# Attention and experts on one core: gate logits of two tiles one round later, loads held to their round, and the last tiles' copies put ahead of the routing work

## The chip, the core and the metric

The kernel runs on one core of one Trainium2 chip. The metric is the device time of one execution in microseconds (us). Three runs of the kernel before took 263.19, 261.66 and 264.2 us, median 263.19.

The engines are named as in the profile: PE multiplies matrices (PEld is its weight load), DVE is the vector engine, ACT the scalar engine, POOL is GpSimd, SP issues nearly all transfers. Each works through its own instructions in order.

## The reference

Attention with a window, then a mixture of experts over its output:

```
scores = q @ k^T / 8;  keep = key < 8  or  0 <= query - key < 96
scores = where(keep, scores - slope[head] * distance, -1e9)
x = softmax(scores) @ v                      # 4 batches x 8 heads x 768 x 64
logits = x @ w_gate                          # 3072 tokens x 8 experts
e = argmax(logits); gate = softmax(logits)[e]
per expert: keep the 80 tokens of highest gate
out[token] = gate * (relu(x @ w1[e]) @ w2[e]);  all other rows of out are zero
```

All data is float32; w1 is 8 x 512 x 1024, w2 is 8 x 1024 x 512.

## The kernel before, in words

**Attention** takes tiles of 128 queries (24 of them) in 48 rounds `u`, two per tile: a round has four heads. The loop over `u` in `fast_path` writes the order of all five queues out by hand (`manual_schedule`), so that what stands first in the code stands first in its engine's queue. In round u, in this order:

- `scores(u)`: PE multiplies q and k into `ring` (three PSUM buffers, two used per round, L180). Four times, DVE adds the bias and takes the extreme (`ts`, `nm`, L200), and ACT takes the exponential (`pwz`, L204). In between stand `transposes(u - 2)` on PE (into `tp`, L241 to L254, and ACT's copy of half of it to `ta`, L258), `invert(u - 1)` on DVE (`z`, L212 and L213) and `norm(u - 1)` on POOL (L221).
- `logits2` in every fourth round: two transposes (L329) of gate logits that DVE has copied to `ls`, and DVE's sums of them (L358).
- `copied(u - 2)`: DVE copies the other half of `tp` to `ta` (L264). From round 20 on SP then stores a finished piece of x to DRAM (L267).
- `logits1` in every fourth round: PE multiplies two finished tiles `ut` with the gate weights into `lps` (L317), and DVE copies that to `ls` (L321).
- `weigh(u - 3)`: PE multiplies `ta` with v into `pair` (L288, L297). After a tile's second round ACT copies `pair` to `ut` (L311). The next tile's first product overwrites `pair`, and so waits for that copy.
- loads of a later tile (`load_blk`: q and v; `keys`: k), weights and wipes by the table `ASKS`, and a few steps of `routes`: softmax and ranks of a group of tiles (the groups have 6, 6, 6, 4 and 2 tiles), nearly all on DVE. The largest step is `compare` (`cf`, L542).

So the tile pair's logits come right after the copy of its second tile: `logits1` in rounds with u % 4 = 3, `logits2` in rounds with u % 4 = 0.

q, v and k sit in buffers of four tiles (k of two batches). SP issues loads as soon as the buffer is free. A weight quarter (512 KB, `w`) has 16 buffers; the first use of one is held back by a write of one element on POOL (`G.memset(t[:1, :1], 0.0)`, L91), so that SP waits until POOL reaches it.

**The drain** (`DRAIN`) writes the end of the attention out step by step. `t46` and `t47` are transposes and copies of the last two rounds, `w44` to `w47` the products with v, `n47` the last normalisation (split over DVE and POOL by `NORM`), `a1` to `c3` the last logits, `r` a step of routing, `o` one wipe (512 KB of zeros to the output).

**Selection** (`select`) ranks the tokens, finishes x in DRAM and finds the 80 tokens of each expert. **Experts** then gathers them and runs 64 weight quarters through PE: each is split into a high and a low part (ACT L810, DVE L814), and each split asks for the next quarter's load, so that 16 are always held or under way. In `select` the order of SP is left to a scheduler, and it put two wipes that `select` asks for near the start of SP's queue, among the first loads.

Of the kernel before, what the change touches and what calls it, by code (L numbers as in the profile page):

```python
# [22 lines left out]
P = 128  # L23
NB = S // P
# [24 lines left out]

EARLY = "k12 q1 v0 k23 v1 q2 w0 v2"  # L50
ASKS = "- - - - - w ww w ww w w - w - w - w - w - w - www -".split()
HELD, EVERY, AFTER = 2, 3, 2
FROM, INSIDE = 18, 14


DRAIN = (
    "r a1 t45 o o w44 r r r n47 r r a2 t46 r r r r w45 r r r "
    "t47 w46 r b1 w47 r r b2 c1 c2 r r r c x x c3 c c r r y y"
)
NORM = (("V", slice(2, 4)), ("G", slice(0, 2)))  # L60
ROWS = (3, 1, 3, 1, 0, 0, 0)
# [9 lines left out]
def fast_path(tc, a, out, cst, x_dram, inp):  # L71
# [4 lines left out]
    with ExitStack() as ctx:  # L76
# [8 lines left out]
        def load_w():  # L85

            for n, (k, e, c) in enumerate(QUARTERS):
                t = wp.tile([P, DF], F32, tag="w", name=f"w{k}_{e}_{c}")
                raw[k, e, c] = t
                if n < NW:  # L90
                    G.memset(t[:1, :1], 0.0)  # L91
                src = (a["w1"] if k == 1 else a["w2"])[e].rearrange("(c p) f -> p c f", p=P)
                yield nc.sync.dma_start(out=t.rearrange("p (c f) -> p c f", c=k), in_=src[:, k * c:k * c + k])
# [46 lines left out]
        with tc.tile_pool(name="at_sb", bufs=2) as sp, ExitStack() as sctx:  # L140
# [19 lines left out]
            def scores(u):  # L160
                t, g = divmod(u, 2)
                m = TURN[t] % NB
                q, kt = inp.blk[t][0], inp.kts[TURN[t] // NB]
                nm, z, ts, pw = st[u]
# [96 lines left out]
            def copied(u):  # L261
                spot = u - FROM
                ta, tp, n = st[u, "ta"]
                V.tensor_copy(out=ta[:, 1, :n], in_=tp[:, :n])  # L264
                if 0 <= spot < 2 * INSIDE:
                    r = TURN[spot // 2] * P
                    nc.sync.dma_start(  # L267
                        out=x_dram[r:r + P, :].rearrange("p (i g c) -> p i g c", i=2, g=2)[:, :, spot % 2], in_=ta[:, :, n - P:n])
                st[u, "ta"] = ta

            def weigh(u):
                t, g = divmod(u, 2)
                m = TURN[t] % NB
                va, vb = inp.blk[t][1:]
                last = u == nu - 1
# [108 lines left out]
            weights = load_w()  # L384
            ahead = islice(weights, NW)
            wipe = clear()
# [3 lines left out]
            for u in range(nu - 1):  # L390
                if u % 2 == 0:
                    next(keys, None)
                if u == 0:
                    for _ in cst["first"]:
                        pass
                begin(u)
                scores(u)
                if u % 4 == 0 and 8 <= u:
                    logits2(u // 2 - 4, 2)
                if 2 <= u:  # L400
                    copied(u - 2)
                if u == 1:
                    for _ in window:
                        pass
                    for z in pwz:
                        G.memset(z[:, 4 * WH:], 0.0)
                    G.memset(cst["zero"], 0.0)
                if u > 2:
                    for _ in range(3):
                        next(late, None)  # L410
                if u % 4 == 3 and 7 <= u:
                    logits1((u - 7) // 2, 2)
                if 3 <= u:
                    idle(2 if u == 3 else 0)
                    weigh(u - 3)
                if u % 2 == 0 and 3 <= u // 2 + 2 < NT:
                    inp.load_blk(u // 2 + 2)
                if u % 2:
                    for k in ASKS[u // 2]:
                        next(dict(w=ahead, o=wipe).get(k, iter(())), None)  # L420
                routes(4 if u >= 40 else 2 + (u % 4 == 3))
            u = nu - 1
# [3 lines left out]
            def whole(u):  # L426
# [3 lines left out]
            step = dict(  # L430
                o=lambda: next(wipe),
                t45=lambda: copied(u - 2), t46=lambda: whole(u - 1), t47=lambda: whole(u),
                w44=lambda: weigh(u - 3), w45=lambda: weigh(u - 2), w46=lambda: weigh(u - 1), w47=lambda: weigh(u),
# [31 lines left out]
        early = [hip.tile([P, DF], F32R, tag="hi", name=f"early{i}") for i in range(3)]  # L465
        select(tc, cst, lps, psa, pair, gs1, rows, due, raw, early, wipe)
        pctx.close()
        rctx.close()
        assert next(ahead, END) is END
        experts(tc, out, cst, x_dram, inp, raw, weights, lps, early, hip, wipe)  # L470


class Route:
# [26 lines left out]
    def all(self):  # L500
        V, A, lg, ex, eq = self.nc.vector, self.nc.scalar, self.lg, self.ex, self.eq
        yield V.tensor_reduce(out=self.mx, in_=lg, axis=AX.X, op=ALU.min)
        yield V.tensor_tensor(out=ex, in0=self.wide(self.mx), in1=lg, op=ALU.subtract)
        yield V.tensor_tensor(out=eq, in0=lg, in1=self.wide(self.mx), op=ALU.is_equal)
        yield A.activation(out=ex, in_=ex, func=AF.Exp, bias=0.0, scale=1.0)
        yield V.tensor_tensor(out=eq, in0=eq, in1=self.cst["pref"].unsqueeze(1).broadcast_to([P, self.n, E]), op=ALU.mult)
        yield V.tensor_reduce(out=self.m2, in_=eq, axis=AX.X, op=ALU.max)
        yield V.tensor_reduce(out=self.sx, in_=ex, axis=AX.X, op=ALU.add)
# [200 lines left out]

def select(tc, cst, lps, psa, pair, gs1, rows, due, w, early, wipe):  # L710

# [9 lines left out]
    with tc.tile_pool(name="sel2", bufs=2) as s2, tc.tile_pool(name="ps_s", bufs=1, space=PSUM) as ps, \  # L721
            tc.manual_schedule(engines=ORDERED):
        duo = ps.tile([P, 2, 512], F32, name="duo")
# [18 lines left out]
        assert next(tiles, END) is END  # L742
        for _ in islice(wipe, AFTER):
            pass
# [35 lines left out]
def experts(tc, out, cst, x_dram, inp, raw, weights, lps, early, hip, wipe):  # L780
# [5 lines left out]
    with tc.tile_pool(name="ffn", bufs=2) as fp, tc.tile_pool(name="hl", bufs=NLO) as hl, \  # L786
# [143 lines left out]
        def prepare(n, behind=False):  # L930
            for k, e, c in islice(fill, n):
                ready[k, e, c] = split(raw.pop((k, e, c)), DF, f"w{k}_{e}_{c}", behind)
                next(weights, None)
                if nsplit % EVERY == 0:
                    next(wipe, None)

        with tc.manual_schedule(engines=ORDERED | {ET.SP}):
            targets(nc, cst)
            for e in range(E):
                gather(e)  # L940
                if e == 0:
                    prepare(1, True)
            nc.sync.dma_start(out=cst["scl"][:1], in_=xgs[0][:1, :2])
            for n in range(2):
                prepare(n)
# [380 lines left out]
class Inputs:  # L1326
# [37 lines left out]

    def load_q(self, t, ks=slice(0, NP * P)):
        self.nc.sync.dma_start(out=self.q[t % self.NQ][:, ks], in_=self.a["q"][TURN[t]][:, ks])

    def load_v(self, t):
        dma, n, m = self.nc.sync.dma_start, TURN[t], TURN[t] % NB
        va = self.va[t % self.NQ]  # L1370
        if m:
            vb = self.vb[t % self.NQ]
# [3 lines left out]
        else:  # L1376
            vb = None
            dma(out=va, in_=self.a["v"][n])
        self.blk[t] = (self.q[t % self.NQ], va, vb)

    def load_blk(self, t):
        self.load_q(t)
        self.load_v(t)

# [69 lines left out]
```

## Time and profile before

| | |
|---|---|
| median of three runs | 263.19 us |
| profiled execution | 262.77 us, of which the span from the first to the last instruction is 261.1 |
| attention, to the drain | 0 to 133 us |
| drain | 133 to 143.7 |
| selection | 143.7 to 159.8 |
| experts | 159.8 to 255.4 |
| busy | PE 239.1 us, DVE 213.8, ACT 206.1, POOL 105.9 |

The span's own engine totals say little, since the stages have different limits: in the experts PE is busy for 95.48 of 95.60 us, in the attention all of PE, ACT and DVE are busy for more than four fifths of the time. The rows are read by stage, and in the attention by round. A round is found in the trace by its four exponentials on ACT: round 8 begins at 27.7 us, round 24 at 70.9, round 40 at 114.7, so a round lasts 2.70 us in the first of these stretches and 2.74 in the second.

### The profile page before, as it was taken

The numbers are of one execution on the slowest core, as the hardware profiler recorded it, in microseconds if no ns is written. First come the engines' busy times: TensorE is split into PE (matmuls) and PEld (weight loads), VectorE is DVE, ScalarE is ACT, GpSimd is POOL, SyncE is SP. The second block draws the span as 40 slices with busy tenths as digits, with TensorE's granted clock in tenths as the row PEclk, the third lists the DMA queues.
The fourth block names the chain that finished last, engine by engine and source line by source line (L and its number), as shares of the span: only waits on it lengthen the run. The fifth ranks groups of instructions, "written<-read, shape, count | busy, mean of one in ns | idle before, by whom it ended". The sixth has DMA issues, their size and how long they took to land.

```text
span 261.1 us, 9657 instructions
## 1 busy us (share of the span) xinstructions
PE 239.1 (92%) x3587; PEld 168.7 (65%) x3587; DVE 213.8 (82%) x785; ACT 206.1 (79%) x583; POOL 105.9 (41%) x196
## 2 busy tenths in 40 slices
PE   7987988899998999998999889999999999999991
PEld 2565766667676786876766645666666666666660
DVE  4877677988878889787987778999999898999860
ACT  3988789999789998997985555888879898979740
POOL 7675565544445744555561438820000031111211
PEclk9999999999999999999999858999999999999999
DMA  5999639999979999898467646999999999999101
GB/s 172 293 353 319 189 103 312 346 334 316 314 226 302 284 259 300 264 283 271 154 195 274 246 158 201 342 326 403 405 407 410 410 401 395 391 407 336 34 25 36
DMA packets 49086, 73.06 MB, mean 280 GB/s; under 512 B 3688, under 2 KB 23528, under 8 KB 49032
## 3 DMA queue, kind: packets, MB, share of 16 engines
q1 hardware_dynamic: 47864, 69.74, 79.6%
q0 software_dynamic: 1024, 2.62, 3.2%
q8 instruction: 30, 0.49, 0.8%
q14 instruction: 24, 0.20, 0.2%
q10 hardware_dynamic: 144, 0.00, 0.0%
HBM read 58.46 MB, written 13.89 MB: 277 GB/s over the span
## 4 chain that ended last, share of the span: by engine, by line
PE 62%; ACT 18%; DVE 8%; issue 5%; POOL 4%; POOLq 0%; DVEq 0%; ACTq 0%
PE hp L840 17%; PE yp L840 17%; ACT pwz L204 11%; PE ring L180 6%; PE pair L288 6%; PE pair L297 3%; ACT ta L258 3%; ACT ut L311 2%; PE lps L317 2%; DVE ts L200 2%; PE tp L895 2%; PE tp L241 2%; PE lps L591 1%; POOL pwz L221 1%; DVE z L212 1%
## 5 line engine op out<-in xcount | busy, mean ns | idle before, releaser
L204 ACT ACTIVATE pwz<-ts,nm 128x168 f32<-128x168 f32 (+1 forms) x192 | 81.4, 426 | 14.8 <-DVE z L212 12.4
L221 POOL TENSOR_TENSOR pwz<-pwz,z 128x672 f32<-128x672 f32 (+2 forms) x48 | 60.3, 1257 | 56.6 <-DVE z L213 34.4
L200 DVE CUSTOM_DVE_ANT_0 ts<-ring,tab 128x168 f32<-128x168 f32 (+1 forms) x192 | 53.2, 315 | 14.4 <-PE ring L180 13.4
L180 PE MATMUL ring<-kt,q 64*64 64x64 f32 (+3 forms) x1088 | 41.1, 268 | 2.1 <-issue 1.0
L923 POOL DMA_INDIRECT out_dram<-vb,si x8 | 9.5, 1188 | 76.7 <-ACT w_0h L810 39.0
L204 ACT ACTIVATION_READ_ACCUMULATOR pwz<-ts,nm 128x1 f32 x192 | 36.6, 191 | 0.0
L180 PEld LDWEIGHTS ring<-kt,q 64*64 64x64 f32 x1088 | 32.4, 133 | 5.4 <-issue 2.9
L288 PE MATMUL pair<-ta,va 104*64 104x128 f32 (+1 forms) x368 | 30.6, 285 | 3.0 <-ACT ut L311 2.1
L264 DVE COPY ta<-tp 128x512 f32<-128x512 f32 (+2 forms) x47 | 28.7, 611 | 0.0
L288 PEld LDWEIGHTS pair<-ta,va 104*64 104x64 f32 (+1 forms) x368 | 19.3, 136 | 12.1 <-issue 6.3
L258 ACT COPY ta<-tp 128x512 f32<-128x512 f32 (+2 forms) x47 | 23.9, 508 | 0.5 <-ACT pwz L204 0.5
L241 PE MATMUL tp<-ident,pwz 64*128 64x64 f32 x376 | 21.9, 235 | 2.0 <-POOL pwz L221 1.4
L241 PEld LDWEIGHTS tp<-ident,pwz 64*128 64x128 f32 x376 | 15.5, 138 | 9.7 <-POOL pwz L221 4.3
L814 DVE TENSOR_TENSOR w_3l<-w,w_3h 128x1024 fp32r<-128x1024 f32 x16 | 19.5, 1221 | 1.4 <-ACT w_3h L810 1.2
L814 DVE TENSOR_TENSOR w_0l<-w,w_0h 128x1024 fp32r<-128x1024 f32 x15 | 18.3, 1221 | 2.0 <-ACT w_0h L810 2.0
L297 PE MATMUL pair<-ta,vb 64*64 64x64 f32 x640 | 18.8, 230 | 1.1 <-issue 1.1
L297 PEld LDWEIGHTS pair<-ta,vb 64*64 64x64 f32 x640 | 13.1, 133 | 8.1 <-issue 7.9
L814 DVE TENSOR_TENSOR w_1l<-w,w_1h 128x1024 fp32r<-128x1024 f32 x15 | 18.3, 1219 | 0.0
L814 DVE TENSOR_TENSOR w_2l<-w,w_2h 128x1024 fp32r<-128x1024 f32 x15 | 18.2, 1216 | 0.0
L810 ACT CAST w_3h<-w 128x1024 fp32r<-128x1024 f32 x16 | 16.7, 1044 | 0.3 <-PE yp L840 0.3
L810 ACT CAST w_2h<-w 128x1024 fp32r<-128x1024 f32 x15 | 15.8, 1056 | 1.2 <-PE hp L840 1.0
L200 DVE DVE_READ_ACCUMULATOR2_ANT nm<- 128x1 f32 x192 | 15.9, 83 | 0.0
(436 smaller groups left out, 521.9 us busy)
## 6 DMA issues: line engine op xcount, KB each, us to landing
w<-in_w_dram SPq DMA_DIRECT2D x64, 512.0 KB
kt<-in_kT_dram SPq DMA_DIRECT2D x23, 272.0 KB
out_dram<-zero SPq DMA_DIRECT2D x12, 512.0 KB
q<-in_q_dram SPq DMA_DIRECT2D x23, 256.0 KB
vb<-in_vb_dram SPq DMA_DIRECT2D x20, 256.0 KB
va<-in_va_dram SPq DMA_DIRECT2D x20, 208.0 KB
x_dram<-ta SPq DMA_DIRECT2D x28, 128.0 KB
x_dram<-kt SPq DMA_DIRECT2D x6, 256.0 KB
```

Source lines behind the costliest of these rows:

```text
L180: T.matmul(sc[hh][64 * i:64 * i + 64, pp, o:o + e - c], q[h, pr * P + 64 * i:pr * P + 64 * i + 64], kt[h, pr, c0 + c:c0 + e], start=True, ...
L200: V.tensor_tensor_reduce(out=ts[:, j, :w], in0=sc[hh][:, pp, :w], in1=tab, scale=-0.125, scalar=3.0e38, op0=ALU.add, op1=ALU.min, accum_ou ...
L204: A.activation(out=pw[:, j, :w], in_=ts[:, j, :w], func=AF.Exp, bias=nm[:, j:j + 1], scale=-1.0, accum_out=z[:, j:j + 1],)
L221: eng.tensor_tensor(out=p, in0=p, in1=zs.unsqueeze(2).broadcast_to(list(p.shape)), op=ALU.mult)
L241: T.transpose(out=tps[i][:, 64 * j:64 * j + 64], in_=pw[hs[i], o:o + P], identity=ident[hs[i], hs[i]])
L258: A.copy(out=ta[:, 0, :n], in_=tps[0][:, :n])
L264: V.tensor_copy(out=ta[:, 1, :n], in_=tp[:, :n])
L288: T.matmul(up[pp][64 * hh:64 * hh + 64], va[:n, 64 * h:64 * h + 64], ta[:n, :, 64 * j:64 * j + 64], start=g == 0 if t < NT - 1 else pp == ...
L297: T.matmul(up[pp][h, 64 * i:64 * i + 64], vb[k, i, 2 * g + pp, :], ta[k, i, 256 + 64 * pp:320 + 64 * pp], start=False, stop=True, skip_gro ...
L810: A.copy(out=hi, in_=src)
L814: V.tensor_tensor(out=lo, in0=src, in1=hi, op=ALU.subtract)
L840: T.matmul(ps, p, q, start=first and i == 0, stop=last and i == 2, skip_group_check=True)
```

## The change

- **Logits one round later.** `logits1` moves from rounds with u % 4 = 3 to those with u % 4 = 0, `logits2` from u % 4 = 0 to u % 4 = 1. The steps of routing that follow them move too: before, four steps were made in each round from 40 on; now five are made in each from 41 on.
- **Loads to their round.** Up to round 20, q and v of a tile are held by a write of one element on POOL, as weights are. v is asked for three rounds later than before (v of tile t in round 2t - 1), k after q instead of ahead of the scores (and, up to round 20, two rounds later).
- **Weights and wipes.** Weight quarters are asked for one at a time from round 5 on, every second round up to round 19, where before they began in round 11. Fourteen are loaded by the end of the drain, two more after the last rows of x; before, all sixteen were. The two wipes that stood near the start are now in rounds 23 and 31. In the experts the first split no longer asks for a quarter: the stream of quarters begins behind the first gather.
- **The drain.** ACT copies the second half of round 46 instead of DVE; the copies of rounds 46 and 47 stand ahead of the routing of the group of four; two small routing operations of that group move from DVE to POOL; the last normalisation has three heads on DVE and one on POOL, instead of two and two.

```diff
-EARLY = "k12 q1 v0 k23 v1 q2 w0 v2"
-ASKS = "- - - - - w ww w ww w w - w - w - w - w - w - www -".split()
-HELD, EVERY, AFTER = 2, 3, 2
+EARLY = "k12 q1 v0 k23 v1 q2 w0"
+ASKS = "- - w w w w w w w w - o - w - o - w - - w - - -".split()
+HELD, EVERY, AHEAD, LATE = 2, 3, 14, 2
+HOLD = 20
 DRAIN = (
-    "r a1 t45 o o w44 r r r n47 r r a2 t46 r r r r w45 r r r "
-    "t47 w46 r b1 w47 r r b2 c1 c2 r r r c x x c3 c c r r y y"
+    "w r w a1 t45 w o w44 o r r r n47 r r a2 t46 r r r w45 t47 r r r r w46 b1 r r r w47 b2 c1 c2 "
+    "r r r c x x c3 c c c r r y y"
 )
-NORM = (("V", slice(2, 4)), ("G", slice(0, 2)))
+NORM = (("V", slice(1, 4)), ("G", slice(0, 1)))
...
-                V.tensor_copy(out=ta[:, 1, :n], in_=tp[:, :n])
+                (A.copy if u == nu - 2 else V.tensor_copy)(out=ta[:, 1, :n], in_=tp[:, :n])
...
             for u in range(nu - 1):
-                if u % 2 == 0:
-                    next(keys, None)
...
-                if u % 4 == 0 and 8 <= u:
-                    logits2(u // 2 - 4, 2)
+                if u % 4 == 1 and 9 <= u:
+                    logits2((u - 9) // 2, 2)
...
-                if u % 4 == 3 and 7 <= u:
-                    logits1((u - 7) // 2, 2)
+                if u % 4 == 0 and 8 <= u:
+                    logits1((u - 8) // 2, 2)
...
                 if u % 2 == 0 and 3 <= u // 2 + 2 < NT:
-                    inp.load_blk(u // 2 + 2)
+                    inp.load_q(u // 2 + 2, hold=u < HOLD)
+                    for _ in range(1 + (u == 20)):
+                        next(keys, None)
                 if u % 2:
+                    if 2 <= u // 2 + 1 < NT:
+                        inp.load_v(u // 2 + 1, hold=u < HOLD)
...
-                routes(4 if u >= 40 else 2 + (u % 4 == 3))
+                routes(5 if u > 40 else 2 + (u % 4 == 3))
...
+        side = self.nc.gpsimd if self.t0 == NT - GROUPS[-2] - GROUPS[-1] else V
-        yield V.tensor_tensor(out=ex, in0=self.wide(self.mx), in1=lg, op=ALU.subtract)
+        yield side.tensor_tensor(out=ex, in0=self.wide(self.mx), in1=lg, op=ALU.subtract)
...
-        for _ in islice(wipe, AFTER):
+        for _ in late:
             pass
...
                 ready[k, e, c] = split(raw.pop((k, e, c)), DF, f"w{k}_{e}_{c}", behind)
-                next(weights, None)
+                if not behind:
+                    next(weights, None)
...
-    def load_q(self, t, ks=slice(0, NP * P)):
+    def load_q(self, t, ks=slice(0, NP * P), hold=False):
+        if hold:
+            self.nc.gpsimd.memset(self.q[t % self.NQ][:1, :1], 0.0)
```

How the orders move, at three places. On PE, in a round with u % 4 = 3 (round 23; `tp` are the transposes, `lps` the gate logits, `pair` the products with v, `ring` the next scores), before:

```order
L254 MATMUL tp_21_1606<-ident,ut_379 128x64
L254 MATMUL tp_21_1607<-ident,ut_379 128x64
L317 MATMUL lps<-ut_1368,wgn 32x256 x4
L288 MATMUL pair<-ta_1541,va 64x128 x4
L297 MATMUL pair<-ta_1541,vb_118 64x64 x8
L180 MATMUL ring_208<-kt_113,q_109 64x128
```

And of the change, in that round:

```order
L255 MATMUL tp_21_1618<-ident,ut_375 128x64
L255 MATMUL tp_21_1619<-ident,ut_375 128x64
L289 MATMUL pair<-ta_1554,va 64x128 x4
L298 MATMUL pair<-ta_1554,vb_118 64x64 x8
L181 MATMUL ring_206<-kt_113,q_109 64x128
```

The four logits products are gone from it: `pair` now follows the transposes at once. They stand in the next round, where the transposes of `ls` (L329) stood:

```order
L255 MATMUL tp_22_1681<-ident,ut_618 128x64
L255 MATMUL tp_22_1682<-ident,ut_618 128x64
L318 MATMUL lps<-ut_1375,wgn 32x256 x4
L289 MATMUL pair<-ta_1620,va 64x128 x4
L298 MATMUL pair<-ta_1620,vb_118 64x64 x8
```

The transposes of `ls` go one round further, into the round with u % 4 = 1, in the same place ahead of `pair`.

On SP, the loads of rounds 4 to 7 of the change (`q`, `kt` and `va`, `vb` are a tile's q, k and v; `w` is a weight quarter):

```order
L1384 DMA vb_119<-in_vb_dram 128x512
L94 DMA w_0_0_495<-in_w_dram 128x1024
L1374 DMA q_110<-in_q_dram 128x512
L1364 DMA kt_113<-in_kT_dram 128x4x136
L1383 DMA va<-in_va_dram 104x512
L1384 DMA vb_116<-in_vb_dram 128x512
L94 DMA w_0_1_622<-in_w_dram 128x1024
```

Before, no weight stood here, q and v of a tile stood together, and two wipes were among them.

On ACT, the end of the drain (`kt` is the place of the last copies), before:

```order
L258 COPY ta_3297<-tp_46_3295 128x256
L505 ACTIVATE ex_3053<-ex_3053 128x32
L311 COPY kt_113<-pair 128x4x128
L258 COPY kt_114<-ring_208 128x256
L309 COPY kt_113<-u_3338 128x2x128
```

And of the change:

```order
L259 COPY ta_3311<-tp_46_3309 128x256
L265 COPY ta_3311<-tp_46_3310 128x256
L312 COPY kt_113<-pair 128x4x128
L259 COPY kt_114<-ring_206 128x256
L508 ACTIVATE ex_3129<-ex_3129 128x32
L310 COPY kt_113<-u_3352 128x2x128
```

The exponential of the routing goes behind two copies, and one copy has come over from DVE.

## Rows read from the trace of the kernel before

**Rows 1.** Busy time by stretch: from:to us, length, PE PEld DVE ACT POOL, clock, DMA share, GB/s.
```profile
27.70:70.90 43.20, 39.43 (x964) 29.92 (x960) 35.83 (x208) 38.60 (x154) 23.34 (x42) 1.00 0.88 276
159.80:255.40 95.60, 95.48 (x476) 62.86 (x476) 86.78 (x95) 77.08 (x101) 18.55 (x13) 1.00 0.89 331
```
**Rows 2.** The chain that ended last, in order of time: start us, us, what.
```profile
89.09 0.48 ACT ut L311
89.61 0.64 PE lps L317 x8
90.25 0.59 PE pair L288 x8
91.23 0.67 PE ring L180 x14
```
**Rows 3.** PE's waits from 27 to 135 us: us in total, times, longest.
```profile
PE lps L317 <- ACT ut L311: 3.3, 7, 0.7
PE pair L288 <- ACT ut L311: 1.4, 6, 0.4
PE ring L180 <- issue: 1.0, 1, 1.0
PE pair L288 <- issue: 0.8, 1, 0.8
```
**Rows 4.** Timeline of rounds 31 and 32, ACT and PE: start us, us, instruction, idle before.
```profile
92.38 0.43 ACT L204 ACTIVATE pwz<-ts,nm 128x168 f32<-128x168 f32 x1 [0.65 <-DVE z L212]
92.48 0.44 PE L329 MATMUL lps<-ident,ls 128*128 128x128 f32 x2
```
**Rows 5.** Timeline of rounds 35 and 36, DVE and ACT.
```profile
102.12 1.08 DVE L542 TENSOR_TENSOR cf<-sx,kval 128x254 bf16<-128x254 f32 x3
103.54 0.43 ACT L204 ACTIVATE pwz<-ts,nm 128x168 f32<-128x168 f32 x1 [0.86 <-DVE z L212]
```
**Rows 6.** PE's waits over the whole run, the one more that "issue" ended.
```profile
PE pair L297 <- issue: 1.1, 1, 1.1
```
**Rows 7.** Busy time by stretch, as in rows 1: three stretches of the early loads.
```profile
6.00:26.00 20.00, 17.01 (x321) 11.54 (x321) 15.37 (x89) 17.94 (x75) 13.29 (x32) 1.00 1.06 322
44.00:58.00 14.00, 12.31 (x306) 9.18 (x300) 12.40 (x71) 13.26 (x55) 7.43 (x13) 1.00 1.02 339
24.00:27.00 3.00, 1.93 (x56) 1.43 (x48) 1.49 (x8) 1.63 (x8) 1.21 (x2) 1.00 1.01 259
```
**Rows 8.** DMA issues on the page: what, count, KB each.
```profile
w<-in_w_dram SPq DMA_DIRECT2D x64, 512.0 KB
kt<-in_kT_dram SPq DMA_DIRECT2D x23, 272.0 KB
...
q<-in_q_dram SPq DMA_DIRECT2D x23, 256.0 KB
vb<-in_vb_dram SPq DMA_DIRECT2D x20, 256.0 KB
va<-in_va_dram SPq DMA_DIRECT2D x20, 208.0 KB
```
**Rows 9.** POOL's holds of weights: durations ns min/median/max, first and last start us.
```profile
L91 POOL MEMSET w<- x16: 88/88/90, 37.4 to 131.0; 1x1 f32 x16
```
**Rows 10.** The page's DMA queues: packets, MB, share of 16 engines' span.
```profile
q8 instruction: 30, 0.49, 0.8%
```
**Rows 11.** Timeline of the drain, POOL, PE and ACT.
```profile
137.31 0.76 POOL L221 TENSOR_TENSOR pwz<-pwz,z 128x256 f32<-128x256 f32 x1 [0.48 <-DVE z L213]
...
138.13 0.46 PE L241 MATMUL ring<-ident,pwz 64*128 64x64 f32 x8
...
138.55 0.23 ACT L505 ACTIVATE ex<-ex 128x32 f32<-128x32 f32 x1 [1.04 <-DVE ex L503]
138.69 0.57 ACT L311 COPY kt<-pair 128x512 f32<-128x512 f32 x1
...
139.89 0.66 PE L288 MATMUL ring<-kt,va 128*64 128x128 f32 x8 [0.15 <-DVE oh L552]
```

More of the change, by code (lines that the diff above doesn't have):

```diff
@@ L89, in load_w @@
                 raw[k, e, c] = t
-                if n < NW:
+                if n < AHEAD:
                     G.memset(t[:1, :1], 0.0)
@@ L162, in scores @@
                 m = TURN[t] % NB
[L163 removed]
+                q, kt = inp.q[t % inp.NQ], inp.kts[TURN[t] // NB]
                 nm, z, ts, pw = st[u]
@@ L273, in weigh @@
                 m = TURN[t] % NB
-                va, vb = inp.blk[t][1:]
+                va, vb = inp.blk[t]
                 last = u == nu - 1
@@ L384, in fast_path @@
             weights = load_w()
-            ahead = islice(weights, NW)
+            ahead = islice(weights, AHEAD)
             wipe = clear()
@@ L430, in fast_path @@
             step = dict(
-                o=lambda: next(wipe),
-                t45=lambda: copied(u - 2), t46=lambda: whole(u - 1), t47=lambda: whole(u),
+                w=lambda: next(ahead), o=lambda: next(wipe), t45=lambda: copied(u - 2), t46=lambda: whole(u - 1), t47=lambda: whole(u),
                 w44=lambda: weigh(u - 3), w45=lambda: weigh(u - 2), w46=lambda: weigh(u - 1), w47=lambda: weigh(u),
@@ L465, in fast_path @@
         early = [hip.tile([P, DF], F32R, tag="hi", name=f"early{i}") for i in range(3)]
-        select(tc, cst, lps, psa, pair, gs1, rows, due, raw, early, wipe)
+        select(tc, cst, lps, psa, pair, gs1, rows, due, raw, early, islice(weights, LATE))
+        assert len(raw) == AHEAD + LATE
         pctx.close()
         rctx.close()
-        assert next(ahead, END) is END
         experts(tc, out, cst, x_dram, inp, raw, weights, lps, early, hip, wipe)
@@ L501, in all @@
         V, A, lg, ex, eq = self.nc.vector, self.nc.scalar, self.lg, self.ex, self.eq
+        side = self.nc.gpsimd if self.t0 == NT - GROUPS[-2] - GROUPS[-1] else V
         yield V.tensor_reduce(out=self.mx, in_=lg, axis=AX.X, op=ALU.min)
-        yield V.tensor_tensor(out=ex, in0=self.wide(self.mx), in1=lg, op=ALU.subtract)
+        yield side.tensor_tensor(out=ex, in0=self.wide(self.mx), in1=lg, op=ALU.subtract)
         yield V.tensor_tensor(out=eq, in0=lg, in1=self.wide(self.mx), op=ALU.is_equal)
         yield A.activation(out=ex, in_=ex, func=AF.Exp, bias=0.0, scale=1.0)
-        yield V.tensor_tensor(out=eq, in0=eq, in1=self.cst["pref"].unsqueeze(1).broadcast_to([P, self.n, E]), op=ALU.mult)
+        yield side.tensor_tensor(out=eq, in0=eq, in1=self.cst["pref"].unsqueeze(1).broadcast_to([P, self.n, E]), op=ALU.mult)
         yield V.tensor_reduce(out=self.m2, in_=eq, axis=AX.X, op=ALU.max)
@@ L707, in search, with select @@
     yield rk[:1, E * NT:E * NT + E]
-def select(tc, cst, lps, psa, pair, gs1, rows, due, w, early, wipe):
+def select(tc, cst, lps, psa, pair, gs1, rows, due, w, early, late):
     nc = tc.nc
@@ L721, in select @@
     with tc.tile_pool(name="sel2", bufs=2) as s2, tc.tile_pool(name="ps_s", bufs=1, space=PSUM) as ps, \
-            tc.manual_schedule(engines=ORDERED):
+            tc.manual_schedule(engines=ORDERED | {ET.SP}):
         duo = ps.tile([P, 2, 512], F32, name="duo")
@@ L943, in experts @@
             nc.sync.dma_start(out=cst["scl"][:1], in_=xgs[0][:1, :2])
+            for _ in islice(weights, NW - AHEAD - LATE):
+                pass
             for n in range(2):
@@ L1363, in keys, with load_v @@
             yield self.load_k(b, slice(0, NP), KB * m, KB * m + KB)
-    def load_q(self, t, ks=slice(0, NP * P)):
+    def load_q(self, t, ks=slice(0, NP * P), hold=False):
+        if hold:
+            self.nc.gpsimd.memset(self.q[t % self.NQ][:1, :1], 0.0)
         self.nc.sync.dma_start(out=self.q[t % self.NQ][:, ks], in_=self.a["q"][TURN[t]][:, ks])
-    def load_v(self, t):
+    def load_v(self, t, hold=False):
         dma, n, m = self.nc.sync.dma_start, TURN[t], TURN[t] % NB
         va = self.va[t % self.NQ]
+        if hold:
+            self.nc.gpsimd.memset(va[:1, :1], 0.0)
         if m:
@@ L1378, in load_v @@
             dma(out=va, in_=self.a["v"][n])
[L1379 to L1383, printed above, removed]
+        self.blk[t] = (va, vb)
 def build(tc, a, out):
```

## The prediction

> **What bounds the kernel now.** I read the busy time by stretch first, then the chain that ended last, then PE's waits, and only then single rounds in the timeline. The stretches say where a change can count at all: in the experts PE is busy for 95.48 of 95.60 us, while in the attention PE is busy for 39.43 of 43.20 us, ACT for 38.60 and DVE for 35.83 [rows 1]. So the attention has no single bound: PE idles 3.77 us in sixteen rounds, and ACT and DVE have little more room. There a gain can only come out of waits. The chain shows one turn of that stage: ACT copies `ut`, PE starts the logits products 0.04 us after the copy's end (89.09 + 0.48 = 89.57, then 89.61), then `pair`, then the next scores, which feed DVE and ACT again [rows 2]. The waits put a sum on it: from 27 to 135 us PE waits 3.3 us in seven places with the logits products, and 1.4 us in six places with `pair`, for the copy of `ut` [rows 3]. And after such a round ACT in turn starves, 0.65 us at 92.38, since the scores came late [rows 4].
>
> **Logits one round later.** No work is added or removed: eight products of 0.64 us in all [rows 2] and two transposes of 0.44 us [rows 4] per four rounds. What moves is who waits.
> In a round with u % 4 = 3, `pair` comes where the logits came, and must wait for the same copy, since it overwrites what the copy reads. So that wait does not go by itself. But behind it 0.64 us are gone from the way to the next scores, which is as long as ACT's idle time of 0.65 us there; the round after it takes the 0.64 us and gives up the 0.44. ACT is thus ahead of PE by up to 0.44 us (what left the way to the scores of the round with u % 4 = 1) when the two light rounds come, and the next copy of `ut` is earlier against PE. A typical wait there is 3.3 / 7 = 0.47 us. I take half of the 3.3 us, 1.65, because ACT's lead passes through DVE, which is nearly as busy.
> In a round with u % 4 = 1, PE now does the transposes of `ls`, 0.44 us, ahead of `pair`, as long as the longest wait there (0.4): the 1.4 us go.
> Sum: -3.0 us. Bounds: -4.7, both waits gone, and +0.5, if the round that now holds the logits is late at DVE as round 36 was (below).
>
> **Routing.** A step of `compare` costs a third of 1.08 us; in rounds 23 and 35 three of them follow the copy `ls` in one round, and ACT then waits 0.86 us instead of 0.65 [rows 4, 5]. In the change one of the three stands a round earlier than the other two. That is worth the difference, 0.2, twice: -0.4 us (bounds 0 and -0.9, half of the 0.86 in each round). From round 41 on, the last group of six has one round less and five steps instead of four; DVE has that work in both, so I take +0.2 us (0 to 0.6, about one `compare` and a half).
>
> **Loads.** A hold costs POOL 88 ns [rows 9], one or two per round up to round 20; nothing waits for a load in the rounds after the first few, and POOL is busy for 23.34 of 43.20 us [rows 1], so it costs nothing. If that cover is gone, one wait of 88 ns per round gives 18 x 0.09 = 1.6 us. What stands behind a held load on SP's queue is k, v and the weight of the same rounds, all for rounds later on. From round 20 on nothing needs a hold: the stores of x stand between the loads on SP's queue and wait for DVE's copies of their round, so SP is paced in both kernels.
> What may go is another wait. Three times PE stood for about 1 us for nothing that the profile shows ("issue"): 1.1 us once, 0.8 and 1.0 later [rows 3, 6]. The first falls between 24 and 27 us, where PE is busy for 1.93 of 3.00 us; the DMA engines are full there, share 1.01, behind twenty microseconds of 1.06 [rows 7]. Instructions come by DMA too, on a queue of their own [rows 10], so a full stretch may hold them up. Here the change takes out two wipes and holds q and v, so I take the first stop as gone and leave the others: -1.0 us. Bounds: -2.9, all three, and +1.0, one more; no row shows the cause. The Trainium skill speaks against this term: "DMA: Bandwidth & Descriptors", section "Queues, rings and completion order", says that each DMA engine takes the queues that have work in turn, packet by packet, so that a long line on SP's queue would hardly hold up a short transfer on another, such as a piece of the program. By that rule the pacing frees no such stop, and the sum would be 1.0 us higher; by the row it stays. No run here shows yet which it is.
> Weights up to the drain are fourteen instead of sixteen; the two left over (1 MB) follow the last rows of x, when the engines have little else. They are the fifteenth and sixteenth quarter to be split, so nobody waits for them. In the experts the stream of quarters starts one quarter later. PE has 0.12 us idle in that stage and 0.89 of the DMA share is used [rows 1]; I cost it at nothing. If that cover is gone, because the line of sixteen runs dry, each quarter late costs PE what it is late; 48 of them, 25 MB, are loaded there.
>
> **Drain.** Before, POOL takes 0.76 us for two heads and ends at 138.07; PE's transposes wait for it and start at 138.13. One head takes about half, 0.38, and ends at 137.7. But the row shows no idle time of PE before its transposes, so PE was not free much earlier, and only 0.1 us goes there. Then ACT's copy of `pair` starts at 138.69 behind an exponential for which ACT idled 1.04 us; the logits, and behind them the last product (139.89), wait for it [rows 11]. With that exponential behind the copies, ACT does one copy of 0.38 more, and starts the copy at about 138.1 instead of 138.69. Of these 0.6 us PE, whose products between are next, lets about 0.4 through. Sum: -0.5 us (bounds -1.0 and +0.3, if POOL's two small operations hold up the routing's last steps, which are the next to be late).
>
> **Sum.** 262.77 (the profiled execution) - 3.0 - 0.4 + 0.2 - 1.0 - 0.5 = 258.1 us. The median of the runs is 0.42 us above that execution: 258.5 us.
>
> **Rivals.**
> *The waits only change places.* `pair` waits as long as the logits did, ACT is no earlier because DVE is the next to end last (round 35 shows it [rows 5]), and only a third of the 1.4 us goes. Then: -0.5 - 0.2 + 0.2 - 0.3 for logits, routing and drain and half a stop, -0.5: 262.77 - 1.3 + 0.42 = 261.9. For it: ACT and DVE are busy for 89% and 83% of the stretch. Against it: the 0.64 us lie on the chain itself.
> *The stops of PE stay or come elsewhere.* That is also what the rule on the queues would give. 258.5 + 1.0 = 259.5. For it: two of the three stops come after 27 us [rows 3], behind the first crowd of loads, and no row shows their cause.
> *The loads become the bound, and it is slower.* From round 5 to 19 two rounds ask for a q, a k, a va, a vb and a weight: 256 + 272 + 208 + 256 + 512 = 1504 KB [rows 8], 1.54 MB in two rounds of 2.6 us, 296 GB/s. The same kinds of transfers ran at 322 and 339 GB/s, with the engines full, but at 259 in one stretch [rows 7]. At 259 two rounds take 5.95 us, 0.75 too long, 6.0 us after eight pairs. A load is asked for four rounds ahead (q of tile t in round 2t - 4, v in 2t - 1 for a product in 2t + 3), 10.4 us, so PE sees that only if eight pairs fall behind by more: from 1.54 MB in 5.2 + 1.3 us on, 237 GB/s. At 215 GB/s two rounds take 7.2 us, the eight fall 15.7 us behind, PE waits 5.3 us, and half of the gain in the logits and all of that in the stops is lost: 262.77 + 5.3 - 1.5 - 0.4 + 0.2 - 0.5 + 0.42 = 266.3. Against it: no row of this mix is that slow. For it: a single queue in order, and v with three rounds less in hand.
> *The pacing does not pace.* SP was held up by buffers anyway; then the loads cost and bring nothing, which is the second rival again.
>
> **How the numbers follow.** The forecast has 0.39, the stops that stay 0.25, the waits that change places 0.27, the loads as bound 0.09. The likeliest time is 258.5; its own range, from the bounds of its terms taken together, is 256 to 260.5. Both signs are not evenly held, three of the four cases are faster. To leave out no more than 2 in 10, the range goes from 255.7 (both waits and two stops gone) to 262.6 (past the case of waits that change places); the slow case stays out. A measurement of this kernel tells 1% (2.6 us: 260.6 and 265.8) from no change. Faster by more: nearly all of the first two cases and a tenth of the third, 0.37 + 0.22 + 0.03 = 0.62. Within: 0.29. Slower: 0.09.
>
> **What would show it.** Right: PE's waits for `ut` and `kt` copies with `pair` and `lps` together at some 2 us from 27 to 135, none of them with `lps`; sixteen rounds in about 42 us; no "issue" stop near 25 us; DMA share under 1 from 10 to 26 us; the drain shorter by half a microsecond; the experts at 95.6. Wrong: waits of PE for transfers of q, k or v (the loads), waits with `pair` of 4 us (changed places), or ACT waiting for DVE's `z` for as long as before, 12 us.

## The result, and the profile after

The changed kernel took 258.44 us (median of four runs, 257.25 to 259.51) against 262.43 for the kernel before, run beside it (261.08 to 264.2): a ratio of 0.9873, 95% interval 0.9829 to 0.9917. The forecast was 258.5. Ratios, here and below, compare the executions within 1.5% of a kernel's fastest. The profiled execution took 259.51 us, its span is 257.7 (before 261.1).

Where the 3.4 us of the span went, by the first exponential of a round on ACT and by PE's first instruction of a stage:

| stretch | before | after | difference |
|---|---|---|---|
| start to round 8 | 27.68 | 26.48 | -1.20 |
| rounds 8 to 24 | 43.21 | 43.00 | -0.21 |
| rounds 24 to 40 | 43.83 | 42.67 | -1.16 |
| rounds 40 to 47 | 19.80 | 19.53 | -0.27 |
| round 47 to the end of the drain | 9.17 | 8.73 | -0.44 |
| selection | 16.15 | 16.31 | +0.16 |
| experts to the end | 101.21 | 100.96 | -0.25 |

The stretches of after that answer to [rows 1, 7], with rounds 24 to 40 in one more row (columns as there):

```profile
6.00:26.00 20.00, 18.56 (x352) 12.40 (x350) 15.18 (x90) 17.96 (x75) 13.66 (x40) 1.00 0.74 207
...
26.48:69.48 43.00, 39.44 (x960) 29.83 (x958) 35.28 (x206) 38.98 (x153) 23.66 (x52) 1.00 0.99 296
69.48:112.15 42.67, 41.13 (x1036) 32.42 (x1036) 37.26 (x210) 40.08 (x153) 22.23 (x26) 1.00 0.94 288
...
156.70:252.00 95.30, 95.28 (x476) 62.93 (x476) 86.81 (x95) 77.02 (x100) 19.00 (x13) 1.00 0.90 333
```

The loads are paced: the DMA share from 6 to 26 us is 0.74 where it was 1.06. What was not loaded there is loaded behind it, at 0.99 up to round 24. In rounds 24 to 40 PE idles 1.54 us (before 2.83). PE's waits from 26 to 132 us, for [rows 3]:

```profile
PE pair L289 <- ACT ut L312: 2.4, 5, 0.7
PE pair L289 <- issue: 1.2, 2, 0.8
PE lps L601 <- DVE lg L359: 0.5, 1, 0.5
PE ring L181 <- DMA kt<-in_kT_dram: 0.4, 1, 0.4
PE pair L289 <- ACT kt L312: 0.4, 1, 0.4
...
PE lps L318 <- ACT kt L312: 0.2, 1, 0.2
```

Of the 5.1 us that PE waited for ACT's copies of `pair` (3.3 + 1.4 in [rows 3], and the 0.4 below) 3.0 are left, nearly all with `pair`. ACT's waits for DVE's `z` have halved; those for `nm` went from 0.5 to 1.1 us. Two lines of before, then one of after:

```profile
PE lps L317 <- ACT kt L311: 0.4, 2, 0.2
...
ACT pwz L204 <- DVE z L212: 12.4, 17, 2.1
...
ACT pwz L205 <- DVE z L213: 6.0, 13, 1.0
```

Two things in PE's waits are new: 0.4 us for a load of k, and 0.5 us for DVE in the routing. The stop near 25 us is gone, one of 0.8 us near 64 us stays, one of 0.4 has come, and the one near 119 us is gone.

### The profile page after: what moved, and what is told of

Read it like the earlier page. It is cut to its first block, busy times and chain, and to the rows that moved or that the text cites. A ratio compares the mean times of both kernels' runs of the same rounds, so it can differ in the third digit from the quotient of the medians.

```text
span 257.7 us, 9711 instructions
## 1 busy us (share of the span) xinstructions
PE 239.6 (93%) x3587; PEld 169.2 (66%) x3587; DVE 213.7 (83%) x782; ACT 208.0 (81%) x584; POOL 107.5 (42%) x214
## 4 chain that ended last, share of the span: by engine, by line
PE 63%; ACT 13%; DVE 10%; DMA 4%; issue 4%; POOL 3%; SPq 0%; POOLq 0%; DVEq 0%; ACTq 0%
PE hp L843 17%; PE yp L843 17%; ACT pwz L205 9%; PE ring L181 6%; PE pair L289 5%; PE pair L298 3%; DMA kt<-in_kT_dram 3%; PE tp L242 3%; ACT ta L259 2%; DVE ts L201 2%; POOL pwz L222 2%; PE tp L898 2%; PE lps L318 1%; DMA q<-in_q_dram 1%; PE lps L330 1%
```

## What the runs were to tell apart

The theory of the prediction has three parts: the logits take waits out of the loop (-3.0, with routing -3.2), full DMA engines cause PE's stops (-1.0), the drain gives 0.5. Its rivals: the waits change places, the stops have another cause. From the trace by stage a third reading came up: the last rounds lose to routing. Twelve kernels ran, each beside the kernel before.

**One part at a time.** Logits and routing alone (before, with the conditions of the loop as changed):

```diff
-                if u % 4 == 0 and 8 <= u:
-                    logits2(u // 2 - 4, 2)
+                if u % 4 == 1 and 9 <= u:
+                    logits2((u - 9) // 2, 2)
...
-                if u % 4 == 3 and 7 <= u:
-                    logits1((u - 7) // 2, 2)
+                if u % 4 == 0 and 8 <= u:
+                    logits1((u - 8) // 2, 2)
...
-                routes(4 if u >= 40 else 2 + (u % 4 == 3))
+                routes(5 if u > 40 else 2 + (u % 4 == 3))
```

> The kernel before with the logits (and the steps of routing that follow them) one round later, and nothing else. Theory of the prediction: -3.2 us, about 259.2 (ratio 0.988), and the stops of PE of about 1 us stay. Theory from the traces of both kernels by stage (rounds 8 to 20 shorter by 0.55 us, 24 to 40 by 1.16): the logits are worth about 2 us, ratio 0.992. Rival, the waits only change places: -0.7 us at most, ratio 0.997.

Ratio 1.0004 (0.9943 to 1.0065), which rests on three executions; all twelve took 259.59 to 266.51 us, median 264.57. Neither number was expected. The trace, of an execution of 264.52 us, says why: rounds 24 to 40 take 42.35 us, the gain is there, but PE stopped twice, for 1.1 and 2.3 us, in rounds 20 and 22, and later waited 1.4 us for the second gather of the experts, which the profile of before does not show. So the gain was gone.

The reverse edit, the changed kernel with these lines put back:

```diff
...
-                if u % 4 == 0 and 8 <= u:
-                    logits1((u - 8) // 2, 2)
+                if u % 4 == 3 and 7 <= u:
+                    logits1((u - 7) // 2, 2)
...
```

> The changed kernel with the logits where they were before; loads and drain as changed. Theory of the prediction: -1.5 us against before (loads -1.0, drain -0.5), ratio 0.994. Theory from the traces by stage: -1.2 up to round 8, +0.3 for the keys that come late in round 21, -0.4 for the drain: -1.3 us, ratio 0.995. Rival, the loads bring nothing: -0.5, ratio 0.998. If logits alone and this one add up to the changed kernel (ratio 0.987), the parts are independent.

Ratio 0.9966 (0.9939 to 0.9993), 260.48 us, 259.6 to 261.3 in twelve runs. No stop of PE in its trace; rounds 24 to 40 take 43.82 us, as before. So the parts do not add up: in the whole time the logits' gain shows only where the loads are changed too (0.9873 for both, 0.9966 and 1.0004 for either).

The drain alone (two of its edits):

```diff
...
-NORM = (("V", slice(2, 4)), ("G", slice(0, 2)))
+NORM = (("V", slice(1, 4)), ("G", slice(0, 1)))
...
-                V.tensor_copy(out=ta[:, 1, :n], in_=tp[:, :n])
+                (A.copy if u == nu - 2 else V.tensor_copy)(out=ta[:, 1, :n], in_=tp[:, :n])
...
```

> The kernel before with the drain, the last normalisation, the copy of the last round but one and the two routing operations as changed; the two wipes of the drain stay there, no weights are added to it. Theory of the prediction: -0.5 us (0.998), to be seen between the last round's first exponential and the end of the attention. Rival: the drain's waits come out again behind POOL's two small operations, 0 to +0.3 us.

Ratio 1.0029 (0.9988 to 1.0070): the whole time doesn't resolve half a microsecond. In the trace the drain takes 8.72 us (9.17 before), as in the changed kernel.

**What of the loads matters.** Without the holds:

```diff
-HOLD = 20
+HOLD = 0
```

> The changed kernel without the holds of q and v on POOL up to round 20; all else as changed. Theory of the prediction (a full stretch of the DMA engines made the stop of PE near 25 us): the DMA share from 6 to 26 us goes back to 1, a stop of about 1 us comes back in rounds 6 to 9, and the time is 1 us above the changed kernel. Rival (the stops hang on where in PE's program a piece of it is asked for, not on the DMA engines): no stop near 25 us, and the keys of round 21, which the holds kept back, come in time: 0.4 us below the changed kernel. Rival (SP is held up by buffers anyway): same time and same DMA share.

Ratio 0.9843 (0.9789 to 0.9898), 258.29 us: no worse than with them. The share from 6 to 26 us is 0.87, not 1, and there is no stop there. PE waits 0.59 us for k in round 39. So the holds of q and v are not needed for the gain.

The two wipes taken from the start, in the kernel with the logits alone:

```diff
-ASKS = "- - - - - w ww w ww w w - w - w - w - w - w - www -".split()
-HELD, EVERY, AFTER = 2, 3, 2
+ASKS = "- - - - - w ww w ww w w o w - w o w - w - w - www -".split()
+HELD, EVERY, AFTER = 2, 3, 0
```

> The kernel before with the logits one round later, and of the loads only the two wipes (512 KB each) taken from the start of SP's queue to rounds 23 and 31; weights, q, k and v asked for as before, no holds. It is compared with logits alone, whose runs were 259.6 to 266.5 us with stops of PE of 1.1 and 2.3 us near 60 and 65 us. Theory A (each stop is a piece of PE's program that came late behind a full line of transfers, wherever the line is from): the stretch from 10 to 26 us is eased a little, the one at 45 to 70 us, where most weights are asked for two at a time, is not; stops near 60 to 65 us stay in most runs, median 262 to 264.5. Theory B (the two wipes at the start were the cause): no stop anywhere, 259 to 260 us.

263.61 us in the median of twelve, ratio 1.0062 (1.0029 to 1.0094), five stops of 5.6 us in all. So taking the wipes from the start does not free the stops by itself.

No weights and no wipes during the attention, again with the logits alone (a `w` in `DRAIN` asks for a weight):

```diff
-ASKS = "- - - - - w ww w ww w w - w - w - w - w - w - www -".split()
+ASKS = "- - - - - - - - - - - - - - - - - - - - - - - -".split()
...
-    "r a1 t45 o o w44 r r r n47 r r a2 t46 r r r r w45 r r r "
+    "r w w w w a1 t45 w w w44 w w r r r n47 r w w r a2 w w t46 w w w w r r r r w45 r r r "
...
```

> The kernel before with the logits one round later, and with no weight and no wipe loaded or stored during the attention: all sixteen weights are asked for in the drain, the wipes after it. Theory A (late pieces of the program behind a crowd of transfers): no stop of PE over 0.2 us between 8 and 130 us, round 47 begins at 130.5 to 131.5 us; what comes after (selection, experts) may be later, since the weights are, and is not what this run is for. Rival (the stops hang on the place in PE's program): the stop in round 22 of about 0.8 us stays. The rounds 24 to 40 show the logits by themselves: 42.4 us or less, where they were 43.8.

The whole takes 273.58 us, since PE then waits 11.9 us for a weight. Its attention is the clean experiment. Two stretches of it:

```profile
6.00:26.00 20.00, 16.61 (x321) 11.54 (x321) 15.16 (x90) 17.98 (x75) 13.34 (x32) 0.99 1.06 276
28.00:130.00 102.00, 97.57 (x2384) 75.38 (x2383) 87.68 (x501) 93.67 (x363) 54.86 (x72) 0.98 0.68 201
```

In the first, full of q, k and v alone, PE stopped for 1.69 us, in round 7. In the second, at a share of 0.68, there is no stop, not even in rounds 20 and 22: the place in PE's program alone does not make it. Rounds 24 to 40 take 42.26 us. Round 47 began at 133.2, later than expected, because of the first stop and what it did to the clock (last section).

q, v and k asked for as before, the rest as changed:

```diff
-EARLY = "k12 q1 v0 k23 v1 q2 w0"
+EARLY = "k12 q1 v0 k23 v1 q2 w0 v2"
...
+                if u % 2 == 0:
+                    next(keys, None)
...
-                    inp.load_q(u // 2 + 2, hold=u < HOLD)
-                    for _ in range(1 + (u == 20)):
-                        next(keys, None)
+                    inp.load_q(u // 2 + 2)
+                    inp.load_v(u // 2 + 2)
...
-                        inp.load_v(u // 2 + 1, hold=u < HOLD)
```

> The changed kernel with q, v and k asked for as before: v with q and three rounds earlier, k ahead of the scores and two rounds earlier up to round 20, one v more at the start, no holds. Weights, wipes, logits and drain as changed. Theory A (stops of PE are pieces of its program that come late behind a crowd): the DMA share from 6 to 26 us goes from 0.74 (with holds) and 0.87 (without) back to 1.05, a stop of 1 to 1.7 us comes back in rounds 6 to 9, and the time is 1 to 2 us above the changed kernel: 259.5 to 260.5. Rival (it is the weights by twos that make the crowd that matters): no stop, time as the changed kernel, 258.4.

258.39 us, all six between 258.26 and 258.71, ratio 0.9851 (0.9807 to 0.9895). The share was less full than before, and the stop did not come:

```profile
6.00:26.00 20.00, 17.87 (x364) 12.71 (x366) 15.72 (x92) 18.12 (x76) 13.39 (x34) 1.00 0.98 281
```

The rival's time came out, 258.4, though the trace has a stop of 1.03 us in round 38: neither the holds of q and v nor the later q, v and k are needed. What is left of the change to the loads is the table of weights (one at a time from round 5 on, each held by its own write on POOL, which also holds up what stands behind it on SP) and the two wipes in later rounds, which brought nothing by themselves. SP's longest wait from 6 to 30 us in this kernel is for such a write:

```profile
SPq L94 <- POOL w L92: 4.6, 2, 3.0
```

That the table is the effective part follows by leaving out the others; no kernel ran with the table alone, and none of the changed ones has the wipes back at the start.

All traces together. "Stops" is what the view of waits gives as "issue" for PE from 8 to 132 us, "loads" what PE waited there for q or k:

| kernel | share 6 to 26 us | stops, us | loads, us |
|---|---|---|---|
| before | 1.06 | 2.9 | 0 |
| logits alone | 1.06 | 3.4 | 0.3 |
| drain alone | 1.07 | 1.3 | 0 |
| wipes later | 1.05 | 5.6 | 0 |
| no weights in the attention | 1.06 | 1.7 | 0 |
| changed | 0.74 | 1.2 | 0.4 |
| without logits | 0.77 | 0 | 0.3 |
| no holds | 0.87 | 0.5 | 0.6 |
| tail back | 0.77 | 0 | 0 |
| no holds, tail back | 0.82 | 1.1 | 0.6 |
| paced tail | 0.76 | 0.2 | 1.0 |
| q, v, k as before | 0.98 | 1.0 | 0 |
| first split asks | 0.75 | 0.2 | 0 |
| q, v, k as before, paced tail | 0.95 | 0.9 | 0 |

Five kernels with a share of 1.05 or more stop for 3.0 us in the mean, nine with less for 0.6, and lose 0.3 to loads that come late. In the first 28 us four of the five stopped, none of the nine. But the five are also all those with the old loads, so the share itself is not shown to be the cause. From 46 to 66 us the four kernels that keep the old weights have 1.04 or 1.05, and each has a stop of PE at 59 to 68 us; of the other ten, at 0.59 to 1.03, two have. A share just below 1 is harmless by itself: the kernel where the first split asks has 0.96 and 0.98 in rounds 8 to 24 and 24 to 40, and 0.2 us of stops.

**The last rounds.** First the logits and the routing of the last tiles put back:

```diff
-                if u % 4 == 1 and 9 <= u:
-                    logits2((u - 9) // 2, 2)
+                if u % 4 == 1 and 9 <= u < 39 or u in (40, 44):
+                    logits2((u - 8 - (u < 39)) // 2, 2)
...
-                routes(5 if u > 40 else 2 + (u % 4 == 3))
+                routes(4 if u >= 40 else 2 + (u % 4 == 3))
```

> The changed kernel with the logits of the last tiles (rounds 39 to 44) and the routing behind them in the rounds where they stood before: logits in rounds 39 and 43, transposes in 40 and 44, four steps of routing per round from 40 on. Theory (rounds 40 to 47, which took 19.3 us undisturbed in the changed kernel and 18.75 in kernels with the old order, lose by the five steps of routing): those rounds take 18.75 to 19.0 us, and the kernel is 0.5 to 0.9 us faster than the changed one, ratio to before about 0.984. Theory of the prediction (+0.2 us for the routing, and the new order worth 0.3 in these rounds): no gain, or a loss of 0.1.

Ratio 0.9854 (0.9801 to 0.9907), 258.6 us: no gain over the changed kernel. Rounds 40 to 47 took 19.54 us, not 18.75. So the logits' place is not what costs there.

And the same without the holds:

```diff
-HOLD = 20
+HOLD = 0
```

> As the one before, and without the holds of q and v up to round 20. If the holds cost nothing and bring nothing, the same time as with them, 257.5 to 258 us; if they keep k back (0.45 us of wait in round 21 of the changed kernel), 0.4 us less; if they free a stop near 25 us, 1 us more.

0.9896 (0.9849 to 0.9942), 260.04 us; with a stop of 1.1 us and 0.6 for q. It tells nothing more of the holds.

What both still had in common with the changed kernel is one round with all three `compare` steps behind the copy `ls`. DVE in round 44 of the changed kernel, and ACT behind it:

```profile
124.70 0.42 DVE L322 COPY ls<-lps 128x256 f32<-128x256 f32 x1
125.03 1.08 DVE L545 TENSOR_TENSOR cf<-sx,kval 128x254 bf16<-128x254 f32 x3
...
126.46 0.43 ACT L205 ACTIVATE pwz<-ts,nm 128x168 f32<-128x168 f32 x1 [0.43 <-DVE z L213]
```

So the steps were shared out as before, with the tail back (the lines against that kernel):

```diff
-                routes(4 if u >= 40 else 2 + (u % 4 == 3))
+                routes(6 if u == 40 else 4 if u > 40 else 2 + (u % 4 == 3))
```

> The changed kernel with the logits of the last tiles where they stood before (as in the run with the tail back) and the steps of routing shared out as the kernel before had them from round 41 to the drain: six in round 40, then four per round, so that one, then two compares fall into rounds 43 and 44 and not three into one. Theory (the +0.8 us of rounds 40 to 47 come from three compares behind the copy of the logits in one round): those rounds take 18.75 us instead of 19.54, the drain is 8.7 us instead of 9.3 of the run with the tail back, and the time is about 1.2 us below that run and below the changed kernel by 0.7: 257.2 to 257.8. Rival (DVE is full there, and the steps cost wherever they stand): no gain.

Rounds 40 to 47 take 18.80 us, as expected. The time does not show it: 259.17 us (257.36 to 261.23), ratio 0.9866 (0.9805 to 0.9927); its trace, of the execution of 261.23 us, has a wait for k of 1.05 us. With the edit of q, v and k as before added, where such waits were not seen:

```diff
...
-                    inp.load_q(u // 2 + 2, hold=u < HOLD)
+                    inp.load_q(u // 2 + 2)
+                    inp.load_v(u // 2 + 2)
...
```

> The changed kernel with q, v and k asked for as before (no holds; that kernel ran in 258.3 to 258.7 us), and with the logits of the last tiles and the routing behind them in the rounds where they stood before, the steps shared out as in the paced tail. Theory (no transfer of q, k or v is waited for, and rounds 40 to 47 are 0.75 us shorter): rounds 40 to 47 in 18.8 us instead of 19.5, no wait of PE for a DMA, 257.6 us, ratio to before 0.981, tighter than the paced tail alone (257.4 to 261.2). Rival: the waits for k and the stops come as they do in the paced tail alone, 259 us.

18.81 us again, with the compares apart (DVE, rounds 43 and 44):

```profile
121.07 0.41 DVE L544 TENSOR_TENSOR cf<-sx,kval 128x254 bf16<-128x254 f32 x1
...
123.59 0.75 DVE L544 TENSOR_TENSOR cf<-sx,kval 128x254 bf16<-128x254 f32 x2
```

257.96 us (257.39 to 263.76), ratio 0.9859 (0.9808 to 0.9909). It has the lowest median but one execution of 263.76 us; against the changed kernel no difference is shown.

**The experts.**

```diff
-                if not behind:
-                    next(weights, None)
+                next(weights, None)
```

> The changed kernel with the one line of the experts undone: the first split again asks for the next weight quarter, ahead of the gathers on their way. In three of four kernels with the old loads PE waited 1.1 to 1.4 us for the second gather near 163 us, and in one of five with the new loads 0.3 us. Theory (the quarter asked for there holds up the gather): a wait of about 1 us for the second gather comes back, 259 to 259.5 us. Theory of the prediction (nothing in the experts): no change, 258.4.

258.89 us (257.75 to 260.85), ratio 0.9883 (0.9829 to 0.9937), with one wait:

```profile
PE xf L835 <- DMA kt<-x_dram,gi: 0.7, 1, 0.7
```

The wait for the second gather came back at two thirds of what was expected, but the time doesn't differ from the changed kernel's, and the kernel without logits had 0.3 us of it without this line. Inconclusive.

## Why the prediction was right, point by point

**The sum: right, in part by luck.** 258.44 us against 258.5 looks closer than it is. The forecast was a fall of 4.7 us; the medians fell by 4.0 and the profiled executions by 3.3, and 258.5 / 263.19 = 0.982 lies just outside the interval of the measured ratio. The kernel before had a median of 263.19 when the forecast was made and 262.43 beside the changed one. And the terms were added up, while the runs show that they depend on each other: by the ratios loads and drain together are worth 0.9 us with the old order of the logits (0.9966 against 1) and 3.4 with the new one (0.9873 against 1.0004).

**Logits: right, nearly to the size.** Taking for each four rounds from 8 to 40 the shortest among the kernels of one order, so that stops and late loads are left out, the old order takes 86.3 us and the new one 83.2: -3.1. The routing in rounds 23 and 35 is part of this number, so the forecast for it is -3.0 - 0.4 = -3.4; the two were not run apart. Two kernels with the same loads show it as well, the one without the logits and the one whose first split asks: rounds 8 to 40 in 86.82 and 83.64 us. PE's waits for ACT's copy there, two lines of the old order (without the logits), then one of the new:

```profile
PE lps L318 <- ACT ut L312: 3.5, 8, 0.6
PE pair L289 <- ACT ut L312: 1.5, 6, 0.4
...
PE pair L289 <- ACT ut L312: 2.4, 5, 0.7
```

So the wait did go to `pair`, but more of it than the forecast took (2.4 us, not 1.65), and PE's waits for POOL, 0.6 us in the old order, went too, which the forecast did not have. In the times, with the loads changed, the logits are worth 0.9966 - 0.9873, or 2.4 us, which fits -3.1 and the +0.8 of the next point. The pair of profiled executions before and after shows only 1.4 in these rounds, since the changed kernel lost 2.5 us there against the shortest rounds, in stops, in waiting for k and in what followed them, and the kernel before 0.7. That ACT's lead would not get through DVE, the rival, is refuted by the 12.4 us that became 6.0.

**Routing at the end: mis-sized.** The term "+0.2 us (0 to 0.6)" measured +0.78: 18.75 us for rounds 40 to 47 in the old order without stops (10.86 + 7.89, without logits), 19.53 in the new one. Five steps per round brought three compares into one round, the very case that [rows 5] shows as round 35; the forecast used those rows for rounds 23 and 35 and did not follow where the third group's compares would fall.

**Loads: right in sign, for the wrong part.** The step said that holding q and v and taking out the wipes frees the stop near 25 us, -1.0. The stop went, the first 26 us are 1.2 us shorter. But it went without the holds and with q, v and k asked for as before too, and taking the wipes out was not enough; what the nine kernels with the changed loads, none of which has that stop, still share is the table of weights, beside the moved wipes, and the step did not name it as a cause. Over all traces the stops fell from 3.0 to 0.6 us, so later stops are part of it as well, though not surely: the changed kernel still has the one in round 22. The term's other half, that nothing behind a held load is waited for, was wrong by 0.45 us, and a wait of PE for k is one of the prediction's own signs of being wrong. The chain of waits of after shows it, from a hold to PE:

```profile
53.72 0.10 POOL q L1373
53.82 0.02 issue
53.84 0.33 SPq L1374
54.17 0.05 issue
54.22 7.79 DMA kt<-in_kT_dram
62.01 0.14 issue
62.15 0.86 PE ring L181 x12
```

POOL's write lets SP issue q in round 18, k follows it, and needs 7.79 us at a share of about 1, to be waited for in round 21. So loads were close to a bound, as the rival said, at a tenth of its price (5.3 us). The hold is not needed for it: without holds, but with v and k asked for as late, PE waited 0.59 and 0.64 us for k and for q; in the two kernels that ask for q, v and k as before it never waited.

The rival from the Trainium skill ("DMA: Bandwidth & Descriptors", "Queues, rings and completion order": the engines take queues in turn, packet by packet, so pacing would free no stop) did not hold for the stops: with the loads paced they are fewer. With its premise the trace agrees: a 16 KB piece of PE's program takes 0.9 to 1.3 us in most cases, in full stretches and in empty ones. What delays the start of a piece is not shown.

**Drain: right.** -0.44 against -0.5. The rows for [rows 11]:

```profile
134.47 0.68 POOL L222 TENSOR_TENSOR pwz<-pwz,z 128x128 f32<-128x128 f32 x1 [0.57 <-DVE z L214]
135.21 0.50 PE L242 MATMUL ring<-ident,pwz 64*128 64x64 f32 x8
135.26 0.58 ACT L312 COPY kt<-pair 128x512 f32<-128x512 f32 x1 [0.32 <-PE pair L298]
...
136.59 0.66 PE L289 MATMUL ring<-kt,va 128*64 128x128 f32 x8
```

From the start of round 47 ACT's copy comes 0.59 us earlier (3.58 against 4.17; 0.6 was forecast), the last product 0.46 (4.91 against 5.37; 0.4). One step was wrong but cheap: one head on POOL takes 0.68 us, not half of 0.76.

**Experts: nothing, as costed.** PE is busy for 95.28 of 95.30 us. In three kernels with the old loads PE did wait 1.1 to 1.4 us for the second gather; the profile before shows no such wait, so what the change is worth there stays open.

## What to carry to other kernels

A gain in a loop counts only while nothing else stops the engine: here the same edit gave 2.4 us of the whole time or nothing, depending on how the loads were spread, so read the stops before judging a change by its time. When steps are moved in a round robin, look in which round the longest ones meet; sharing them out as one and then two took rounds 40 to 47 from 19.54 to 18.80 us. A hold on a queue in order holds everything behind it: follow the next load, not only the held one.

## What the hardware showed

**Stops and pieces of the program.** All nineteen stops of 0.3 us or more that the traces have between 8 and 132 us end 2.4 to 3.1 us after a 16 KB piece began to move on the instruction queue (before: 23.64 and 26.18, 63.16 and 65.75, 117.57 and 120.22 us). Pieces begin about 5 us apart, so that is no chance. They move no slower in those cases (0.9 to 1.7 us), so it seems that they begin late. Whether they are asked for late or wait for a turn the trace doesn't tell. The place counts too: twelve of the nineteen stops fall in rounds 7, 20 and 22. The Trainium skill ("Runtime: NRT & Kernel Launch", "Instruction fetch mechanics") calls the cost of a new block mostly hidden; if the stops are that cost, up to 2.3 us of it was not hidden here.

**After a stop the clock can stand at half.** With no weights in the attention, around its stop (PE's granted clock is the third number from the end):

```profile
24.00:26.00 2.00, 0.71 (x19) 0.40 (x15) 1.30 (x7) 1.68 (x8) 1.26 (x2) 0.89 1.06 266
26.00:28.00 2.00, 1.60 (x30) 1.35 (x29) 0.00 (x0) 0.00 (x0) 0.00 (x0) 0.50 0.80 230
28.00:30.00 2.00, 2.00 (x23) 1.07 (x24) 1.84 (x12) 1.53 (x6) 1.16 (x1) 0.50 0.05 17
```

PE was busy for 0.71 of 2 us, then the clock stood at the lower level, 1.2 GHz, until about 32 us; round 8 took 4.68 us instead of 2.74. The paced tail's wait for k of 1.05 us did the same: 0.53 and 0.62 from 58 to 62 us, and round 20 took 4.33 us instead of 2.96. Stops of 0.8 to 1.1 us in the kernel before left the clock at 1.00. The length of the stop alone does not decide it: in the kernel with the wipes later one of 0.78 us was followed by the lower level, one of 1.70 was not. So one stop costs its length, or that and, in the round behind it, 1.9 or 1.4 us more in these two cases, which would fit the spread between executions (260.0 to 266.1 us for the kernel before); only profiled executions show it.
